# Chunk-selected attention into top-1 routed experts on one core: the last weight piece and two token tiles are sent for sooner, and the last output tile is made in two halves

## The chip, the cores and the metric

The kernel runs on one core of one Trainium2 chip. TensorE (PE) multiplies matrices, and its weight loads are listed apart as PEld. VectorE is DVE, ScalarE is ACT, GpSimd is POOL and SyncE is SP. SP, ACT and POOL also send transfers off; such a row is marked SPq, ACTq or POOLq, or carries the name of a DMA operation, and all transfers run on the same 16 DMA engines. The metric is the device time of one launch in microseconds (us), and lower is better.

## What is computed

The first half is an attention in which each query uses only six chunks of 32 keys, and the second half sends each token through one of eight experts. In the reference, cut to what matters:

```python
ub = sum(maximum(q*k_min[chunk], q*k_max[chunk]))     # bound of each chunk, causal chunks only
top_chunks = argsort(ub)[..., -6:]
attn = softmax(where(sel & causal, q @ k.T / 8, -1e9)) @ v     # 4 batches, 8 heads, 768 tokens, 64 wide
x = attn.transpose(0, 2, 1, 3).reshape(3072, 512)
expert_idx = argmax(x @ w_gate, axis=1)               # 8 experts
for e in range(8):
    xe = x[expert_idx == e]
    out[expert_idx == e] = gate_w * (maximum(xe @ w1[e], 0) @ w2[e])   # 512 -> 1024 -> 512
```

## The kernel before

**Attention.** The work goes by pairs of heads, 16 pairs, four of them to a batch. When the four pairs of a batch are done, a few small steps on DVE choose each token's expert, and six indirect transfers of POOL (line 500, steps `s0` to `s5`) scatter the rows of that batch to a table in DRAM, `xs_dram`, sorted by expert.

**Experts.** The tokens are taken in tiles of 128 rows of one expert. 26 tiles, j = 0 to 25, are always computed. The first 20 are whole tiles; of those the first ten hold rows of the first three batches alone, so they can begin before the last batch is scattered. The last six are made of two halves of 64 rows that belong to two experts. For one tile the steps are:

- `g`: a small transfer, from ACT's queue, of each row's gate and number (line 718);
- `x`: a transposing transfer, from SP's queue, of the tile's rows, 128 by 512 numbers of two bytes (line 743);
- `U`: 16 or fewer matrix products of x with w1 into a two-bank PSUM tile `ph` (line 783);
- `Rl`: ReLU on ACT, from `ph` to the buffer `h` (line 792); there are two buffers `h`;
- `H`: a transposing transfer, from SP's queue, of `h` to `hT` (line 802);
- `D`: products of `hT` with w2 into `py` (line 809), eight for a whole tile and 16, on two halves of the array's columns, for a tile of two experts;
- `Y`: ACT scales `py` by the gate into `y` (line 816);
- `O`: POOL sends the rows of `y` to the output by an indirect transfer (line 820).

**Weights.** w1 and w2 are loaded in 32 pieces of 512 KB by transfers of POOL's queue (line 182, steps `w.0` to `w.31`), which read four-byte numbers and write two-byte ones. `w.26`, `w.14` and `w.30` are the last three that are issued, and all three are pieces of w2. Which expert a whole tile belongs to is known only at run time, so its products read w1 and w2 at an offset from a register. Therefore U.0 waits for every piece of w1, and D.0 for every piece of w2.

**Order.** The text `ORDER` (lines 872 to 943) sets the order of all steps by hand. Each engine issues its instructions, and each queue its transfers, in that order. A transfer takes part in it at the place of its step, so an `x` that stands behind an `H` in the text is issued by SP behind that `H`, which waits for its ReLU. A ReLU writes one of two buffers `h`, so Rl.3 waits until the transfer H.1 has read the buffer that Rl.1 wrote, and Rl.4 until H.2 has.

The waits that the program sets by semaphores, as far as they matter here: U.j waits for x.j and for a free `ph` of three; D.j waits for H.j and for a free `py`; D.0 waits for H.0 and for all of w2; Y.j waits for D.j; O.j for Y.j.

Of the kernel before, what the change touches and what calls it, by code (L numbers as in the profile page):

```python
# [22 lines left out]
def kernel(  # L23
# [18 lines left out]
    DM = H * D  # L42
# [12 lines left out]
    NS = NA + NL + ND + NF2  # L55
# [14 lines left out]
    w2_all = wpool.tile([128, E * WE], BF16)  # L70
# [27 lines left out]
    ps_s = tc.alloc_tile_pool(name="ps_s", bufs=3, space=bass.MemoryType.PSUM)  # L98
    ps_o = tc.alloc_tile_pool(name="ps_o", bufs=1, space=bass.MemoryType.PSUM)
# [17 lines left out]
    for c in range(2):  # L117
# [3 lines left out]
        a = const.tile([128, S], BF16, name=f"IND{c}")  # L121
# [4 lines left out]
    for i in range(2):  # L126
        a = buf.tile([128, 2, 32], FP32, name=f"KK{i}")
# [390 lines left out]
    tag_all = const.tile([128, JT, 2], I32)  # L518
# [161 lines left out]
    NFC = F // 128  # L680
# [5 lines left out]
    fs = [dict() for _ in range(NTILE)]  # L686
# [3 lines left out]
    def kind(j):  # L690
        if j < NA + NL:
            return "whole", j
        if j < NA + NL + ND:
            return "mixed", NFULL + NF2 + j - NA - NL
        if j < NS:
            return "first", NFULL + j - NA - NL - ND
        if j < NS + NB - NL:
            return "whole", NA + NL + j - NS
        return "second", NFULL + NF2 + ND + j - NS - NB + NL
# [103 lines left out]
        fs[j]["hT"] = hT  # L803

    def down_mm(j):
        py = ps_o.tile([128, DM], FP32, tag=("oa", "ob")[j % 2], name="py")
        for c in range(NFC):
            for r, wo in fs[j]["gr"]:
                nc.tensor.matmul(py[r], lhsT=fs[j]["hT"][:, c, r], rhs=w2_all[:, ds(wo + c * DM, DM)],  # L809
                                 start=(c == 0), stop=(c == NFC - 1), skip_group_check=True)  # L810
        fs[j]["py"] = py

    def down_act(j):
        tag, pool, bufs = (("v", ld, LDB["v"]), ("ot", work, 2))[j % 2]
        y = pool.tile([128, DM], FP32, tag=tag, bufs=bufs, name="y")
        nc.scalar.activation(y[:], fs[j]["py"][:], AF.Copy, bias=0.0, scale=tag_all[:, kind(j)[1], 0:1].bitcast(FP32))  # L816
        fs[j]["y"] = y

    def put(j):
# [25 lines left out]
    def sm_c(i):  # L845
# [8 lines left out]
              ra=rb_(r_add), rb=rb_(r_max), rc=rb_(r_shift), rx=rb_(r_exp), rd=rb_(r_cand), re=rb_(r_first),  # L854
              rf=rb_(r_hot), rg=rb_(r_sum), rh=rb_(r_eps), ri=rb_(r_gate), rk=rb_(r_rank), rm=rb_(r_row),
              rn=rb_(r_pick), ro=rb_(r_slot), rp=rb_(r_int),
              g=gather, x=x_in, z=idle_mm, xc=x_tag, U=up_mm, Rl=up_act, H=up_turn, D=down_mm, Y=down_act, O=put, dr=lambda n: nc.gpsimd.drain(), sp=pause, wg=load_gate)
    for u in range(6):
        fn.update({f"sc{u}": sg(sc, u), f"ex{u}": sg(ex, u), f"cm{u}": sg(cm, u), f"av{u}": sg(av, u),
                   f"ac{u}": sg(ac, u), f"s{u}": rb_(r_scat, u)})  # L860

    def steps(gen, n, last):
# [85 lines left out]
    for step in ORDER.split():  # L948
        nm, n = step.split(".")
# [6 lines left out]
    with tc.If(more[0] > 0) as _:  # L956
        for j0 in range(NS, NTILE, 3):
            for j in range(j0, min(j0 + 3, NTILE)):
                gather(j)
                x_in(j)  # L960
                x_tag(j)
            for j in range(j0, min(j0 + 3, NTILE)):
                up_mm(j)
                up_act(j)
                up_turn(j)
            for j in range(j0, min(j0 + 3, NTILE)):
                down_mm(j)
                down_act(j)
                put(j)
# [35 lines left out]
```

## Times and profile before

| what | value |
|---|---|
| time, median of 3 runs | 303.07 us (302.65 to 311.62) |
| profiled execution, its own time | 305.6 us |
| span of its trace, first to last instruction | 303.7 us |
| busy share of PE, DVE, ACT, POOL | 94%, 65%, 62%, 53% |
| granted TensorE clock | 0.998 of full speed |
| bytes moved by the DMA engines | 56.51 MB, 186 GB/s over the span |

All times of rows count from the span's start. PE is busy nearly throughout, so what matters is where it is not, and what it waits for there. The share of busy DMA engines that a view by stretches gives may be above 1, since packets of several queues overlap on an engine.

### The profile page before, as it was taken

How to read it: one execution, taken by the hardware profiler on the slowest of the kernel's cores; microseconds unless marked ns; L12 is line 12 of the kernel's file. 1: busy time of each engine (PE TensorE's matmuls, PEld its weight loads, DVE VectorE, ACT ScalarE, POOL GpSimd, SP SyncE). 2: the span in 40 equal slices, each digit the busy share in tenths (PEclk: the TensorE clock that was granted, in tenths of full speed). 3: DMA queues.
4: the chain of work that ended last, by engine and by line, in shares of the span. 5: the costliest groups of instructions: out<-in, count | busy, mean ns of one | idle time of the engine just before them, and what ended most of it. 6: DMA issues, size and time to landing. Idle time of an engine off the chain costs nothing.

```text
span 303.7 us, 8579 instructions
## 1 busy us (share of the span) xinstructions
PE 285.2 (94%) x3095; PEld 145.3 (48%) x3105; DVE 197.0 (65%) x613; ACT 189.3 (62%) x266; POOL 159.5 (53%) x245
## 2 busy tenths in 40 slices
PE   7899999989999999899999999998699999999992
PEld 3444555454555555555655554453344444444451
DVE  6587988989999988899899899776700322000000
ACT  1978877777777787597877677522435453434541
POOL 5064253553262566635578888413864456753453
PEclk9999999999999999999999999999999999999999
DMA  7999999997989999799999898999997999989872
GB/s 152 201 193 202 201 190 210 177 204 167 208 163 160 191 208 211 149 229 171 189 244 204 159 205 194 106 167 149 224 224 176 208 150 210 235 191 228 139 172 77
DMA packets 132587, 56.51 MB, mean 186 GB/s; under 512 B 121915, under 2 KB 121917, under 8 KB 132544
## 3 DMA queue, kind: packets, MB, share of 16 engines
q1 hardware_dynamic: 117440, 29.13, 52.9%
q0 software_dynamic: 12224, 26.78, 44.8%
q10 hardware_dynamic: 2880, 0.02, 1.4%
q8 instruction: 28, 0.46, 0.6%
q14 instruction: 15, 0.12, 0.1%
HBM read 53.26 MB, written 9.99 MB: 208 GB/s over the span
## 4 chain that ended last, share of the span: by engine, by line
PE 61%; DVE 9%; issue 9%; POOL 6%; DMA 5%; ACT 4%; SPq 3%; POOLq 1%; DVEq 0%; ACTq 0%
PE oa L324 16%; PE ph L783 8%; PE py L809 6%; PE ps L288 6%; DVE Pa L335 5%; PE ps L296 5%; PE pc L242 4%; PE pc L352 4%; POOL out_dram L820 3%; PE ob L324 3%; PE pc L362 2%; DMA KQ<-xg 2%; PE pq L208 2%; PE px L199 2%; DMA x_early<-xs_dram 2%
## 5 line engine op out<-in xcount | busy, mean ns | idle before, releaser
L304 ACT ACTIVATE Pa<-ps 128x1024 f32<-128x1024 f32 x64 | 65.1, 1024 | 15.2 <-PE ps L296 10.0
L335 DVE TENSOR_TENSOR Pa<-Pa 128x1024 f32<-128x1024 f32 (+2 forms) x64 | 64.5, 1008 | 6.9 <-PE oa L324 2.2
L324 PE MATMUL oa<-Pa,v 128*64 128x512 f32 (+2 forms) x320 | 64.3, 518 | 0.0
L311 POOL TENSOR_SCALAR_AFFINE_SELECT Pa<-Pa 128x256 f32<-128x256 f32 x48 | 25.1, 538 | 50.0 <-ACT Pa L304 47.4
L809 PE MATMUL py<-w_all,hT 128*128 (+1 forms) x251 | 46.9, 379 | 1.5 <-issue 1.2
L792 ACT ACTIVATE h<-ph 128x1024 bf16<-128x1024 f32 (+1 forms) x27 | 26.5, 990 | 31.5 <-DMA hT<-h 12.7
L288 PE MATMUL ps<-KQ 64*128 64x512 bf16 (+3 forms) x256 | 37.3, 307 | 1.3 <-ACT Pa L304 0.6
L820 POOL DMA_INDIRECT out_dram<-y,tag_all x26 | 25.7, 989 | 22.9 <-ACT y L816 18.6
L500 POOL DMA_INDIRECT xs_dram<-xrow,sli x24 | 27.8, 1156 | 13.4 <-issue 4.8
L296 PE MATMUL ps<-mt,IND 64*128 64x256 bf16 (+4 forms) x512 | 34.4, 225 | 0.2 <-DVE mt L272 0.2
L809 PEld LDWEIGHTS <-hT 128*128 128x128 bf16 (+1 forms) x256 | 20.8, 102 | 26.0 <-issue 3.3
L816 ACT ACTIVATE y<-py,tag_all 128x512 f32<-128x512 f32 x26 | 17.6, 687 | 21.3 <-PE py L809 19.5
L214 DVE TENSOR_REDUCE KK<-pk 128x24 f32<-128x768 f32 x32 | 29.2, 943 | 1.3 <-PE pk L208 1.2
L324 PEld LDWEIGHTS oa<-Pa,v 128*64 128x64 f32 x320 | 19.4, 136 | 19.8 <-issue 14.7
L783 PE MATMUL ph<-w_all,x_early 128*128 (+1 forms) x125 | 25.3, 379 | 3.0 <-DMA x_early<-xs_dram 2.4
L288 PEld LDWEIGHTS <-KQ 64*128 64x128 bf16 x256 | 13.2, 94 | 28.9 <-issue 28.4
L296 PEld LDWEIGHTS <-IND 64*128 64x128 bf16 x512 | 23.0, 94 | 7.5 <-issue 0.4
L311 POOL TENSOR_SCALAR_AFFINE_SELECT Pb<-Pb 128x256 f32<-128x256 f32 x32 | 20.7, 672 | 9.7 <-ACT Pb L304 8.1
L182 POOL DMA_DIRECT2D w_all<-in_moe_w_dram x32 | 23.9, 748 | 0.1
L752 DVE TENSOR_TENSOR tag_all<-tag_all,inv_i 128x1 int32<-128x1 int32 x10 | 1.5, 158 | 31.8 <-DMA tag_all<-xs_dram 28.5
L783 PE MATMUL ph<-w_all,KQ 128*128 (+1 forms) x127 | 21.9, 380 | 0.1
L226 ACT ACTIVATE qN<-pq 128x576 f32<-128x576 f32 x16 | 10.4, 652 | 15.4 <-PE pq L208 15.4
(167 smaller groups left out, 449.7 us busy)
## 6 DMA issues: line engine op xcount, KB each, us to landing
w_all<-in_moe_w_dram POOLq DMA_DIRECT2D x32, 512.0 KB
k<-in_k_dram SPq DMA_DIRECT2D x32, 192.0 KB
q<-in_q_dram SPq DMA_DIRECT2D x32, 192.0 KB
v<-in_v_dram SPq DMA_DIRECT2D x32, 192.0 KB
hT<-h SPq DMA_TRANSPOSE x27
out_dram<-y,tag_all POOLq DMA_INDIRECT x26
xs_dram<-xrow,sli POOLq DMA_INDIRECT x24
tag_all<-xs_dram ACTq DMA_DIRECT2D x20, 1.0 KB
```

The source lines that it names most:

```text
L214: nc.vector.tensor_reduce(KK[i % 2][:, n, 0:NCH], st[i]["pk"].rearrange("p (c w) -> p c w", w=CH), AX.X, ALU.max if n == 0 else ALU.min, n ...
L288: nc.tensor.matmul(ps[:, hd, ds(c0, w)], lhsT=kc_[r, ts(kb_, 128)], rhs=qc_[r, ds(q0, w)], start=True, stop=False, skip_group_check=True)
L296: nc.tensor.matmul(o[:, :, c, :], lhsT=IND[c][r, ts(kb_, 128)], rhs=mt[r, ds(j0, n), :], start=False, stop=True, skip_group_check=True)
L304: nc.scalar.activation(P[:], st[i][f"ps{u}"][:, :, 0:w], AF.Exp)
L311: nc.gpsimd.affine_select(out=pd, in_=pd, pattern=[[0, 2], [1, 128]], compare_op=ALU.is_ge, fill=0.0, base=0, channel_multiplier=-1)
L324: nc.tensor.matmul(po[64 * hd:64 * hd + 64, ds(q0 - o0, w)], lhsT=vt[:, kb_, hd, :], rhs=P[:, hd, ds(c0, w)], start=(u <= 1 and n == 0), s ...
L335: nc.vector.tensor_tensor(a[:, :, ds(q0_, w)], a[:, :, ds(q0_, w)], P[:, :, ds(c0, w)], ALU.add)
L500: d = nc.gpsimd.indirect_dma_start(out=xs_dram[:], out_offset=bass.IndirectOffsetOnAxis(ap=sli[:, u:u + 1], axis=0), in_=bst[b]["xrow"][:, ...
L783: nc.tensor.matmul(ph[r, fh, :], lhsT=fs[j]["xT"][:, c, r], rhs=w1_all[:, ds(wo + c * F + fh * 512, 512)], start=(c == 0), stop=(c == NDC ...
L792: nc.scalar.activation(h_[:, a].rearrange("q a (c j p) -> q (a c) j p", c=2, j=2), fs[j]["ph"][:, a].rearrange("q a (c p j) -> q (a c) j p ...
L809: nc.tensor.matmul(py[r], lhsT=fs[j]["hT"][:, c, r], rhs=w2_all[:, ds(wo + c * DM, DM)], start=(c == 0), stop=(c == NFC - 1), skip_group_c ...
L820: d = nc.gpsimd.indirect_dma_start(out=out[:], out_offset=bass.IndirectOffsetOnAxis(ap=tag_all[:, kind(j)[1], 1:2], axis=0), in_=fs[j]["y" ...
```

## The change

Three edits. In the text of the order, `w.30` stands right behind `w.14` now, ahead of three steps of POOL's own (`lga`) that it was behind; and `x.5` and `x.6` each stand one `H` further ahead: x.5 ahead of H.1 (it was behind H.2), x.6 between H.1 and H.2 (it was behind x.5, behind both). And the last tile's products, j = 25, are computed in two halves of 256 columns, each half in a PSUM bank of its own, from the pool that `ph` comes from; ACT scales each half by itself. There are 32 products of 256 columns in place of 16 of 512, so 16 more weight loads, and two ACT instructions in place of one. The output transfer O.25 stays one.

```diff
     def down_mm(j):
-        py = ps_o.tile([128, DM], FP32, tag=("oa", "ob")[j % 2], name="py")
-        for c in range(NFC):
-            for r, wo in fs[j]["gr"]:
-                nc.tensor.matmul(py[r], lhsT=fs[j]["hT"][:, c, r], rhs=w2_all[:, ds(wo + c * DM, DM)],
-                                 start=(c == 0), stop=(c == NFC - 1), skip_group_check=True)
-        fs[j]["py"] = py
+        if j == NS - 1:
+            ends = ps_s.tile([128, 2, 512], FP32, tag="s", name="py")
+            fs[j]["py"] = ends[:, :, 0:DM // 2]
+        else:
+            fs[j]["py"] = ps_o.tile([128, DM], FP32, tag=("oa", "ob")[j % 2], name="py")[:].unsqueeze(1)
+        n = fs[j]["py"].shape[2]
+        for a in range(DM // n):
+            for c in range(NFC):
+                for r, wo in fs[j]["gr"]:
+                    nc.tensor.matmul(fs[j]["py"][r, a], lhsT=fs[j]["hT"][:, c, r],
+                                     rhs=w2_all[:, ds(wo + c * DM + a * n, n)],
+                                     start=(c == 0), stop=(c == NFC - 1), skip_group_check=True)
 
     def down_act(j):
...
-        nc.scalar.activation(y[:], fs[j]["py"][:], AF.Copy, bias=0.0, scale=tag_all[:, kind(j)[1], 0:1].bitcast(FP32))
+        n = fs[j]["py"].shape[2]
+        for a in range(DM // n):
+            nc.scalar.activation(y[:, ds(a * n, n)], fs[j]["py"][:, a], AF.Copy, bias=0.0,
+                                 scale=tag_all[:, kind(j)[1], 0:1].bitcast(FP32))
...
-        av4.15 av5.15 xr.13 xt.14 ac0.15 lga.13 ac2.15 w.14 Rl.0 ut.14 rcp.14 sm.15 lgt.14 g.1 ocA.15 gt.15 xr.14
-        lga.14 uc.15 g.2 xt.15 ut.15 rcp.15 g.3 lgt.15 g.4 U.1 lga.15 xr.15 ra.15 rb.15 H.0 rc.15 rx.15 rd.15 U.2
-        rg.15 x.4 re.15 rh.15 rf.15 Rl.1 Rl.2 U.3 rk.15 w.30 H.1 ri.15 rm.15 H.2 rn.15 x.5 ro.15 rp.15 U.4 Rl.3 x.6
+        av4.15 av5.15 xr.13 xt.14 ac0.15 lga.13 ac2.15 w.14 w.30 Rl.0 ut.14 rcp.14 sm.15 lgt.14 g.1 ocA.15 gt.15
+        xr.14 lga.14 uc.15 g.2 xt.15 ut.15 rcp.15 g.3 lgt.15 g.4 U.1 lga.15 xr.15 ra.15 rb.15 H.0 rc.15 rx.15 rd.15
+        U.2 rg.15 x.4 x.5 re.15 rh.15 rf.15 Rl.1 Rl.2 U.3 rk.15 H.1 x.6 ri.15 rm.15 H.2 rn.15 ro.15 rp.15 U.4 Rl.3
         Rl.4 x.7 s0.15 D.0 H.3 D.1 s1.15 Y.0 Y.1 tB.0 tB.1 g.5 g.6 g.7 s2.15 H.4 sp.0 U.5 D.2 Rl.5 s3.15 U.6 g.8
```

SP's queue at the start of the expert stage, before. The rows are x.4, H.1, H.2, x.5, x.6, x.7 and H.3; an ISA row sets the address of the x behind it.

```order
L743 DMA_TRANSPOSE x_early_3718<-xs_dram_63 128x4x128
L802 DMA_TRANSPOSE hT_3881<-h_3851 128x8x128
L802 DMA_TRANSPOSE hT_3887<-h_3853 128x8x128
L743 ISA
L743 DMA_TRANSPOSE x_early_3718<-xs_dram_63 128x4x128
L743 ISA
L743 DMA_TRANSPOSE KQ0_124<-xs_dram_63 128x4x128
L743 ISA
L743 DMA_TRANSPOSE KQ0_124<-xs_dram_63 128x4x128
L802 DMA_TRANSPOSE hT_3926<-h_3908 128x8x128
```

The same place of SP's queue in the changed kernel: x.4, x.5, H.1, x.6, H.2, x.7, H.3.

```order
L743 DMA_TRANSPOSE x_early_3718<-xs_dram_63 128x4x128
L743 ISA
L743 DMA_TRANSPOSE x_early_3718<-xs_dram_63 128x4x128
L802 DMA_TRANSPOSE hT_3882<-h_3853 128x8x128
L743 ISA
L743 DMA_TRANSPOSE KQ0_124<-xs_dram_63 128x4x128
L802 DMA_TRANSPOSE hT_3889<-h_3855 128x8x128
L743 ISA
L743 DMA_TRANSPOSE KQ0_124<-xs_dram_63 128x4x128
L802 DMA_TRANSPOSE hT_3926<-h_3909 128x8x128
```

So H.1 has one more x ahead of it and H.2 two; from x.7 on the queue is as it was.

POOL at the same time: the pieces of weights are the rows of line 182, `lga` is line 408, and the scatters of the last batch are line 500.

```order
 L182 DMA w_all<-in_moe_w_dram 128x2x1024
 L408 TENSOR_TENSOR lg<-lg,lgt 128x96
-L182 DMA w_all<-in_moe_w_dram 128x2x1024
+L182 DMA w_all<-in_moe_w_dram 128x2x1024 x2
 L408 TENSOR_TENSOR lg<-lg,lgt 128x96 x2
-L182 DMA w_all<-in_moe_w_dram 128x2x1024
 L500 DMA xs_dram<-xrow,sli 24576x258 x3
```

w.30 has left its place between the two `lga` and the scatters and is the second of the pair behind the first `lga`. PE and DVE keep their order but for the last tile.

## Rows read from the trace of the kernel before

**Rows 1.** Waits of TensorE, 196 to 300 us: total, times, longest (us).

```profile
PE ph L783 <- DMA x_early<-xs_dram: 2.4, 2, 1.8
PE py L809 <- issue: 1.2, 1, 1.2
```

**Rows 2.** Timeline of TensorE: start, length (us), engine, line, tile, count [idle before].

```profile
210.13 1.89 PE L783 MATMUL ph<-w_all,x_early 128*128 x8 [0.31 <-issue]
213.26 3.62 PE L809 MATMUL py<-w_all,hT 128*128 x15 [1.25 <-issue]
218.71 1.89 PE L783 MATMUL ph<-w_all,x_early 128*128 x8 [1.83 <-DMA x_early<-xs_dram]
220.43 1.89 PE L809 MATMUL py<-w_all,hT 128*128 x8
...
225.61 3.62 PE L809 MATMUL py<-w_all,hT 128*128 x15
```

**Rows 3.** Line 809 by itself, waits before weight loads: ns min/median/max, first and last start.

```profile
L809 PEldq EVENT_SEMAPHORE  x2: 51/990/1929, 211.1 to 211.2; - x2
```

**Rows 4.** Timeline of POOL, 196 to 212 us.

```profile
197.26 0.73 POOL L182 DMA_DIRECT2D w_all<-in_moe_w_dram  x1
202.84 0.38 POOL L408 TENSOR_TENSOR lg<-lg,lgt 128x96 f32<-128x96 f32 x1 [4.84 <-DVE lgt L400]
...
205.53 0.72 POOL L182 DMA_DIRECT2D w_all<-in_moe_w_dram  x1
```

**Rows 5.** Timeline of SP's queue in several stretches, 200 to 216 us.

```profile
202.51 3.26 SPq L743 DMA_TRANSPOSE x_early<-xs_dram  x1
207.62 1.24 SPq L802 DMA_TRANSPOSE hT<-h  x1
...
207.62 4.85 SPq L802 DMA_TRANSPOSE hT<-h  x2
212.63 1.19 SPq L743 DMA_TRANSPOSE x_early<-xs_dram  x1
213.96 2.53 SPq L743 DMA_TRANSPOSE KQ<-xs_dram  x2
```

**Rows 6.** Timeline of ACT, 206 to 222 us.

```profile
206.59 1.01 ACT L792 ACTIVATE h<-ph 128x1024 bf16<-128x1024 f32 x1
...
214.01 1.02 ACT L792 ACTIVATE h<-ph 128x1024 bf16<-128x1024 f32 x1 [5.09 <-DMA hT<-h]
216.03 1.02 ACT L792 ACTIVATE h<-ph 128x1024 bf16<-128x1024 f32 x1 [0.99 <-DMA hT<-h]
...
221.67 1.02 ACT L792 ACTIVATE h<-ph 128x1024 bf16<-128x1024 f32 x1 [3.46 <-DMA tag_all<-xs_dram]
```

**Rows 7.** Stretches: length, busy PE, PEld, DVE, ACT, POOL, clock, DMA share, GB/s.

```profile
198.50:205.50 7.00, 6.70 (x80) 3.69 (x80) 5.44 (x16) 2.11 (x3) 0.77 (x2) 1.00 1.22 180
...
211.50:212.50 1.00, 0.52 (x3) 0.02 (x1) 0.86 (x6) 0.00 (x0) 0.69 (x2) 1.00 0.05 5
```

**Rows 8.** Timeline of the end, 289 to 304 us.

```profile
289.31 8.80 PE L809 MATMUL py<-w_all,hT 128*64 x80
...
298.20 0.69 ACT L816 ACTIVATE y<-py,tag_all 128x512 f32<-128x512 f32 x1 [1.04 <-PE py L809]
299.16 0.97 POOL L820 DMA_INDIRECT out_dram<-y,tag_all  x1 [0.76 <-ACTq L956]
```

**Rows 9.** Groups by form, ACT: count, busy us, mean ns, idle before.

```profile
L816 ACT ACTIVATE y<-py,tag_all 128x512 f32<-128x512 f32 x26 | 17.6, 687 | 21.3 <-PE py L809 19.5 <-issue 1.7
L343 ACT ACTIVATE ot<-oa 128x512 f32<-128x512 f32 x16 | 9.6, 601 | 0.7 <-PE oa L324 0.7
L341 ACT ACTIVATE ot<-ob 128x256 f32<-128x256 f32 x16 | 6.4, 398 | 0.0
```

**Rows 10.** Timeline: products of 256 columns, and two loads of 64 columns.

```profile
184.02 0.38 PE L296 MATMUL ps<-mt,IND 64*128 64x256 bf16 x4
...
288.88 0.11 PEld L783 LDWEIGHTS <-x_early 128*64 128x64 bf16 x2
```

## Prediction, written before the changed kernel was run

> **What bounds the kernel now.** I began with the page's busy shares, which put TensorE far ahead of the others, and so asked for TensorE's own waits. From 196 us on, where the experts begin, there are three of any size: two for token tiles and one of 1.2 us in the products with w2 that the view can't name [rows 1]. The timeline gives their places [rows 2]. U.4 starts at 210.13 and ends at 212.02. D.0 starts only at 213.26: that is the wait of 1.25 us. D.0 and D.1 take 1.73 us each and end at 216.88; U.5 starts at 218.71, 1.83 us later, held by x.5. Behind it TensorE goes on without a gap that counts, so work that starts sooner here ends the kernel sooner, if nothing else comes late.
>
> **What D.0 waits for.** One of two waits ahead of line 809's weight loads lasts 1929 ns from 211.2, so until 213.13 [rows 3]. D.0 needs H.0 and all of w2. H.0 was issued long before; the last piece, w.30, was issued at 205.53 [rows 4]. The DMA engines stand nearly still from 211.5 to 212.5 [rows 7], which fits a piece whose bytes have been moved and whose completion is still to come. I take w.30 as the cause, by elimination.
>
> **What x.5 waits for.** SP issues it at 212.63, behind H.1 and H.2 [rows 5]. H.1 can't start before Rl.1 ends, at 207.60 [rows 6], and takes 1.24; the two together take 4.85, so H.2 alone has some 3.5, against 1.24 when nothing holds it. x.4 was slow too, 3.26, and both times weight pieces were moving. In between, from 205.77 to 207.62, SP waits for Rl.1 with nothing to do.
>
> **When the H land.** This isn't recorded, but ACT shows it: Rl.3 reuses the buffer that H.1 reads and starts at 214.01, Rl.4 that of H.2 at 216.03, both held by "DMA hT<-h" [rows 6]. H.1 thus lands at about 213.95, and D.1, which needs it, starts at 214.99 (213.26 and 1.73) [rows 2]. D.1 has 1.0 us to spare, no more. This is the number that decides.
>
> **The change, part by part.**
>
> *w.30 behind w.14.* POOL issues it at 198.0 (197.26 and 0.73) and waits for DVE from there until 202.84 [rows 4], so its 0.72 us of POOL hides in that wait; if the wait were gone, `lga.14` would be later by 0.72 and nobody would notice before the last batch's routing. Nothing waits for the place at 205.53 that it leaves. Its bytes stand behind w.26 and w.14 in the same queue. The engines move 180 GB/s in all from 198.5 to 205.5 [rows 7], 1.26 MB, of which those two pieces alone are 1.05 MB beside token tiles and H.0, so w.30 starts to flow 0 to 2 us sooner, not 7.5. D.0 then starts between 212.02, the end of U.4, and 213.26 as now: a gain of 0 to 1.25 by itself.
>
> *x.5 ahead of H.1.* Its price on SP is between 1.19, its own length now, and 3.26, that of x.4 just ahead of it with pieces moving [rows 5]. x.4 is the nearer in place, the other the nearer in that SP's queue has had time to empty; I take the middle, 2.1. From 205.9 that ends at 208.0, so H.1 is issued 0.4 late. Its 131 KB (128 by 512 by 2 bytes) go ahead of H.1's at 180 GB/s, 0.73 us. H.1 lands at 213.95 + 0.4 + 0.73 = 215.1. D.1 starts then, whether D.0 began at 212.02 or at 213.26: what w.30 gives is lost in the wait for H.1. The other end is 213.75, H.1 no obstacle and D.0 at 212.02.
>
> *U.5* then follows D.1 at once: 215.1 + 1.73 = 216.85 in place of 218.71, a gain of **1.86**. Its `ph` is free after Rl.3, at 215.1 + 1.0, in time. x.5 has been on its way since 206 and is no longer late.
>
> *x.6 ahead of H.2.* H.2 landed at 216.0; with the bytes of x.5 and x.6 ahead, 1.46 us, at 217.5. D.2 needs it at 216.85 + 1.73 = 218.6: covered, with 1.1 to spare. If that cover were gone, each microsecond would show one for one. x.7 and H.3 have the same transfers ahead of them as before; H.3 landed by 221.67, when Rl.5 got its buffer [rows 6], and D.3 would want it at 225.61 - 1.86 = 223.75 [rows 2]. So the gain is kept. Behind this the transfers follow TensorE's own steps and move with it.
>
> *The last tile in halves.* TensorE: five tiles of 16 products take 8.80 [rows 8], 110 ns a product, two side by side. 32 products of 256 columns cost the same if they take 55 ns. Four of 256 columns with a load each took 0.38 [rows 10], of which the length of one such product is most, so about 53 ns apart: I take 0 extra. ACT's part behind the last product, 0.69 now [rows 8], is a half. A plain copy of 512 columns takes 601 and of 256 columns 398 [rows 9], so halving saves 203 ns; bounds are 0 (the first half waits for the last product after all) and 0.34 (half of 687). I take **0.20**. O.25 and its landing stay.
>
> **Sum.** 1.86 + 0.20 = 2.06 us. The profiled execution took 305.6, of which 303.7 span and 1.9 around it: 303.5. The median is 303.07, 2.5 under the profiled one, near the lower of the runs (302.65): less 2.06 that is **301.0**.
>
> **The rivals.**
>
> *All of it (0.18).* H.1 isn't delayed, because w.30 is out of its way sooner and x.5 fits SP's empty 1.85 us. Then D.0 starts at 212.02, D.1 at 213.75 to 213.95 and U.5 at 215.5 to 215.7: 3.0 to 3.2, with the end 3.2 to 3.4, about 299.7. For it: 1.19 is the commoner length. Against: the same bytes move on engines whose share is above 1 all the while [rows 7].
>
> *Little of it (0.17).* x.5 takes 3.26 as x.4 did, until 209.2, and H.1 behind it 3.5 as H.2 did, until 212.7. H.2 landed 3.5 after its issue ended (212.47 to 216.0), so H.1 lands at 216.2, U.5 starts at 217.95: 0.75, with the end 0.95, so 302.1.
>
> *Slower (0.12).* x.5 meets what H.2 met: SP is held until 212.47, when the pieces have gone. H.1 is issued from 212.6 to 213.85 and lands 3.5 to 4 later, at 217.4 to 217.85. The point that decides is 216.98 (218.71 less 1.73): an H.1 later than that is a loss. U.5 starts 0.4 to 0.9 late, and H.2, behind x.6, makes D.2 wait as much again at worst. Less 0.20, it is 0.2 to 1.5 over, about 303.9. For it: two transfers of SP's queue in four were held here. Against: SP has 1.85 us to spare there.
>
> *Weight loads in the open (0.06).* Two loads of 64 columns take 0.11 [rows 10]. If the 16 added ones don't run beside products, the last tile takes 8 times 0.11 = 0.88 longer; with 1.86 and 0.20 gained, 301.9. Against: 16 products with 16 loads come at 110 ns, little over what the columns need, so today's loads are hidden [rows 8]. The Trainium skill (TensorE: Matmul & The Clock Gate, "The mechanism" under "Part 3: Packing small matmuls — row/col tiling") has a rule for this rival: a weight load overlaps products in flight only when it goes to another group of rows, and all loads here use all 128 rows. By that rule the 0.88 is paid; by the trace it isn't, for loads on all rows are hidden in every tile now.
>
> The forecast keeps 0.47.
>
> **Range and chances.** All cases but part of the slower one lie from 299.7 to 303.6; with 0.3 of scatter at the lower end the range is **299.4 to 303.6**. A measurement of this kernel tells about 2%, 6 us, from no change. No case reaches 6 us either way, so within 2% has 0.95, and what is left, faster 0.02 and slower 0.03, is for what I haven't thought of.
>
> **What would show it.** D.0's wait at line 809 shorter; x.5's row on SP at about 205.9 and its length between 1.2 and 3.3; Rl.3, which tells when H.1 lands, at about 215.2; TensorE waiting for H.1 between D.0 and D.1; U.5 at about 216.85 without a wait for its tile; ACT's last instruction some 0.48 long. Wrong would be Rl.3 behind 217, or D.0 still waiting past 213.3 with w.30 issued at 198: then the wait was never for w.30.

## The result, and the profile after

The changed kernel takes 305.02 us (median of 19 runs, 303.03 to 311.34), the kernel before, beside it on the same chip, 303.05 (19 runs, 301.05 to 311.62). The ratio is 1.0065 with a 95% interval of 1.0044 to 1.0086: about 2.0 us slower, where 2.1 us faster was forecast. The profiled execution of the changed kernel took 304.1 us, span 302.2, mean granted clock 0.993, less than that of the kernel before (305.6, span 303.7): one execution of each would have told the wrong sign.

TensorE's waits from 196 to 300 us in the changed kernel, to be laid beside [rows 1]:

```profile
PE ph L783 <- DMA x_early<-xs_dram: 1.8, 1, 1.8
PE py L815 <- ACT y L824: 1.5, 1, 1.5
```

The wait of 1.2 without a name is gone, and so is one of the two for token tiles. A new one, for ACT's `y`, has come. TensorE's timeline, beside [rows 2], tells which they are (line 815 is line 809 of before, and 824 is 816):

```profile
196.67 1.89 PE L783 MATMUL ph<-w_all,x_early 128*128 x8
203.10 3.61 PE L783 MATMUL ph<-w_all,x_early 128*128 x16
208.56 1.89 PE L783 MATMUL ph<-w_all,x_early 128*128 x8 [1.85 <-DMA x_early<-xs_dram]
210.59 1.89 PE L783 MATMUL ph<-w_all,x_early 128*128 x8
212.31 3.62 PE L815 MATMUL py<-w_all,hT 128*128 x16
215.77 1.89 PE L783 MATMUL ph<-w_all,x_early 128*128 x8
219.19 1.89 PE L815 MATMUL py<-w_all,hT 128*128 x8 [1.53 <-ACT y L824]
221.23 3.61 PE L783 MATMUL ph<-w_all,KQ 128*128 x16 [0.16 <-issue]
```

From the top: U.0; U.1 and U.2; U.3, which now waits 1.85 for x.3; U.4; D.0 and D.1 without a wait; U.5 without a wait; D.2, which now waits 1.53 for Y.0; U.6 and U.7.

Why x.3 is late is to be seen in three rows: POOL's timeline (w.14 and w.30 in one row), the chain of waits (start, length, what), and SP's timeline, where H.0 stands in front of x.4 and x.5:

```profile
196.14 1.45 POOL L182 DMA_DIRECT2D w_all<-in_moe_w_dram  x2
```

```profile
196.75 11.28 DMA x_early<-xs_dram
...
213.19 4.25 DMA hT<-h
```

```profile
199.68 4.53 SPq L802 DMA_TRANSPOSE hT<-h  x1
204.35 3.21 SPq L743 DMA_TRANSPOSE x_early<-xs_dram  x2
209.62 2.13 SPq L802 DMA_TRANSPOSE hT<-h  x1
211.89 1.19 SPq L743 DMA_TRANSPOSE KQ<-xs_dram  x1
213.19 1.24 SPq L802 DMA_TRANSPOSE hT<-h  x1
```

x.3 is issued at 196.75, in the midst of w.14 and w.30, and lands 11.28 us later, at 208.03. H.0 takes SP 4.53, where it took 1.58 in the kernel before (and H.1 1.24, [rows 5]). How the third piece holds x.3 is to be seen in the packets that the DMA engines moved. Queue q0 is POOL's, with the weight pieces in packets of 2 KB. Queue q1 is SP's, where the 131 KB of an x go in 512 packets of 256 bytes. These are the packets, MB and shares from 202 to 206 us, while w.14 and w.30 flow, and below them those from 208 to 209, when no piece is left:

```profile
q0 software_dynamic: 363, 0.71, 93.6%
q1 hardware_dynamic: 365, 0.09, 17.4%
...
q1 hardware_dynamic: 1041, 0.26, 131.8%
```

Beside a piece the two queues move packet for packet, about 91 a us each, and so they do elsewhere (after_third, 210 to 214 us: 360 and 358; same_again, 202 to 204: 175 and 172). Alone, SP's queue moves 1041 in one us. From these rows I estimate that an x would need 512 / 91 = 5.6 us with a piece beside it all the time, and half a us without one. The third piece keeps a piece beside x.3 until past 206 us; in same_again the two that flow there have gone by 204.4.

Behind H.1 stands x.6 (the KQ row, 211.89), and H.2 can go only at 213.19. ACT's timeline shows what hangs on both, beside [rows 6]:

```profile
202.19 6.21 ACTq L718 DMA_DIRECT2D tag_all<-xs_dram  x3
208.59 1.92 ACT L792 ACTIVATE h<-ph 128x1024 bf16<-128x1024 f32 x2
213.16 1.02 ACT L792 ACTIVATE h<-ph 128x1024 bf16<-128x1024 f32 x1 [2.66 <-DMA hT<-h]
217.54 1.02 ACT L792 ACTIVATE h<-ph 128x1024 bf16<-128x1024 f32 x1 [3.35 <-DMA hT<-h]
218.46 0.68 ACT L824 ACTIVATE y<-py,tag_all 128x512 f32<-128x512 f32 x1
```

Rl.4 (217.54) waits until H.2 has landed (213.19 + 4.25 = 217.44). Y.0 stands behind it on ACT, at 218.46, and D.2 writes the `py` that Y.0 reads: it starts at 219.19. The first row is a side effect. In the list of instructions with their waits, g.2, g.3 and g.4 wait for the semaphores of x.0, x.1 and x.2 in the kernel before and for those of x.1, x.2 and x.3 in the changed one, since moving x.5 shifts the turn of the eight semaphores that these transfers share. So ACT is held until x.3 has landed, and Rl.1, H.1 and x.6 start later.

The end, beside [rows 8], TensorE, ACT and POOL:

```profile
287.64 8.82 PE L815 MATMUL py<-w_all,hT 128*64 x96
```

```profile
296.55 0.84 ACT L824 ACTIVATE y<-py,tag_all 128x256 f32<-128x256 f32 x2 [1.06 <-PE py L815]
```

```profile
297.67 0.97 POOL L829 DMA_INDIRECT out_dram<-y,tag_all  x1 [0.93 <-ACTq L965]
```

The halves cost TensorE nothing (8.82 against 8.80). But from TensorE's end to the last put it is 297.67 - 296.46 = 1.21, where it was 299.16 - 298.11 = 1.05.

### The profile page after: what moved, and what is told of

The parts are those of the page before. It is cut to its first block, busy times and chain, and to the rows that moved or that the text cites. A ratio compares the mean times of both kernels' runs of the same rounds, so it can differ in the third digit from the quotient of the medians.

```text
span 302.2 us, 8622 instructions
## 1 busy us (share of the span) xinstructions
PE 286.1 (95%) x3121; PEld 146.1 (48%) x3121; DVE 197.8 (65%) x613; ACT 189.2 (63%) x267; POOL 158.2 (52%) x245
## 4 chain that ended last, share of the span: by engine, by line
PE 61%; DVE 12%; DMA 8%; issue 5%; SPq 5%; ACT 4%; POOL 4%; ACTq 0%; POOLq 0%; DVEq 0%
PE oa L324 12%; PE py L815 11%; PE ph L783 11%; DVE Pa L335 6%; PE ps L288 5%; PE pc L242 5%; DMA x_early<-xs_dram 4%; PE ps L296 4%; PE pc L352 3%; PE ob L324 2%; DVE KK L214 2%; SPq L743 2%; DMA k<-in_k_dram 2%; POOL out_dram L829 2%; PE pq L208 2%
## 5 line engine op out<-in xcount | busy, mean ns | idle before, releaser
L335 DVE TENSOR_TENSOR Pa<-Pa 128x1024 f32<-128x1024 f32 (+2 forms) x64 | 65.2, 1019 | 6.2 <-PE oa L324 1.9
L815 PE MATMUL py<-w_all,hT 128*128 (+3 forms) x272 | 47.2, 367 | 1.5 <-ACT y L824 1.5
L792 ACT ACTIVATE h<-ph 128x1024 bf16<-128x1024 f32 (+1 forms) x27 | 26.5, 990 | 27.5 <-DMA hT<-h 14.3
L500 POOL DMA_INDIRECT xs_dram<-xrow,sli x24 | 26.9, 1120 | 16.2 <-DVE cnt L527 7.6
L815 PEld LDWEIGHTS <-hT 128*128 128x128 bf16 (+1 forms) x272 | 21.6, 103 | 25.7 <-issue 3.3
L824 ACT ACTIVATE y<-py,tag_all 128x512 f32<-128x512 f32 (+1 forms) x27 | 17.8, 670 | 21.3 <-PE py L815 20.0
L783 PE MATMUL ph<-w_all,KQ 128*128 (+2 forms) x128 | 21.9, 380 | 0.2 <-issue 0.2
L226 ACT ACTIVATE qN<-pq 128x576 f32<-128x576 f32 x16 | 10.4, 653 | 15.3 <-PE pq L208 15.3
```

The source lines that it names most:

```text
L335: nc.vector.tensor_tensor(a[:, :, ds(q0_, w)], a[:, :, ds(q0_, w)], P[:, :, ds(c0, w)], ALU.add)
L500: d = nc.gpsimd.indirect_dma_start(out=xs_dram[:], out_offset=bass.IndirectOffsetOnAxis(ap=sli[:, u:u + 1], axis=0), in_=bst[b]["xrow"][:, ...
L783: nc.tensor.matmul(ph[r, fh, :], lhsT=fs[j]["xT"][:, c, r], rhs=w1_all[:, ds(wo + c * F + fh * 512, 512)], start=(c == 0), stop=(c == NDC ...
L792: nc.scalar.activation(h_[:, a].rearrange("q a (c j p) -> q (a c) j p", c=2, j=2), fs[j]["ph"][:, a].rearrange("q a (c p j) -> q (a c) j p ...
L815: nc.tensor.matmul(fs[j]["py"][r, a], lhsT=fs[j]["hT"][:, c, r], rhs=w2_all[:, ds(wo + c * DM + a * n, n)], start=(c == 0), stop=(c == NFC ...
```

## The result across executions: the measure for the experiments

Times of two equal kernels differ here by about as much as the edits are worth, so each experiment is also read by a distance within its own trace: from U.0's start to U.8's. The executions begin U.0 between 196 and 207 us, the late ones at a mean granted clock of 0.98 to 0.99; within the stretch a tile takes 1.73 us of TensorE in all of them, so only distances from U.0 are compared. Without any wait the distance would be 27.5 to 28.3 (each row less its waits). "Third piece" is where the last of w.26, w.14, w.30 stands: late (behind rk.15, as before) or early. Ratios are to the kernel before, run beside it on the same chip.

```
kernel          third piece  x.6       waits of TensorE, U.0 to U.8       U.0 to U.8  ratio (95%)
before          late         old       U.4 .31, D.0 1.25, U.5 1.83        31.30
same_again      late         old       D.0 1.60                           29.42       1.0026 (0.9995-1.0057)
halves_only     late         old       D.1 .38, U.5 1.00                  29.17       1.0018 (0.9964-1.0072)
x_only          late         ahead     D.1 .81, D.2 .51                   29.39       1.0036 (0.9989-1.0083)
x_halves        late         ahead     D.0 1.40                           29.01       1.0004 (0.9967-1.0042)
y0_x_halves     late         ahead     U.1 .15, U.2 .79                   28.89       1.0044 (1.0008-1.0080)
x5_halves       late         old       D.0 1.86                           29.48       1.0035 (0.9993-1.0077)
w_swap          late (w.14)  ahead     D.0 .51, D.1 .34                   28.42       1.0026 (0.9990-1.0063)
x5_swap         late (w.14)  old       D.0 1.21                           28.83       1.0016 (0.9979-1.0053)
no_w30          none         ahead     D.2 1.44, U.6 .20                  29.41       0.9975 (0.9937-1.0013)
no_w30_x_back   none         old       U.5 1.65                           29.26       0.9978 (0.9937-1.0019)
x5_no_w30       none         old       U.1 .32, U.8 .33                   28.14       0.9950 (0.9905-0.9995)
after           early        ahead     U.3 1.85, D.2 1.53, U.6 .16        31.47       1.0065 (1.0044-1.0086)
after_again     early        ahead     U.3 .83, D.2 1.30                  30.32       1.0015 (0.9979-1.0052)
after_third     early        ahead     U.3 1.88, D.2 1.53                 31.49       1.0062 (1.0025-1.0099)
w_only          early        old       U.3 2.26, U.5 .35, D.4 .86         31.73       1.0012 (0.9966-1.0058)
w_mid           early        ahead     U.1 .24, U.4 2.98, D.2 .74         31.69       0.9972 (0.9916-1.0027)
w_fourth        early        ahead     U.3 .91, U.4 1.28, D.2 .80         31.01       1.0064 (1.0019-1.0109)
```

The first row, on which the prediction rests, is the only one with a late third piece that is longer than 29.5. All eight ratios with a late third piece lie above 1, at 1.0026 in the mean, and that of the unchanged kernel is among them: a ratio of this size can come from the measure itself.

## The experiments

Edits of the order are given as the few steps around the place. The expectations speak of three theories. A: w.30 right behind w.14 puts three pieces in a row on the DMA engines, and they hold the token tiles back. B: x.5 and x.6 ahead of H.1 and H.2 make Rl.4, Y.0 and so D.2 late. C: the loss is elsewhere, in the halves, in the stages ahead, or in the clock.

**same_again: the kernel before once more, unchanged.**

> The kernel before, unchanged, as one more kernel of the row. It shows how far two equal kernels stand apart (0 expected, an interval of some 0.3% either way), what clock their executions have in the records, and how much the attention stage and the start of the expert stage differ from one profile to the next.

```profile
213.56 3.61 PE L809 MATMUL py<-w_all,hT 128*128 x16 [1.60 <-issue]
217.21 1.89 PE L783 MATMUL ph<-w_all,x_early 128*128 x8
```

TensorE again: D.0 waits 1.60, and U.5 doesn't wait at all. Against itself the kernel reads 1.0026, which is what such a ratio can be off by.

**halves_only: the two functions of the change, the order of before.**

```diff
-lga.13 ac2.15 w.14 w.30 Rl.0
+lga.13 ac2.15 w.14 Rl.0
-x.4 x.5 re.15 ... rk.15 H.1 x.6 ri.15 rm.15 H.2 rn.15 ro.15
+x.4 re.15 ... rk.15 w.30 H.1 ri.15 rm.15 H.2 rn.15 x.5 ro.15 ... Rl.3 x.6
```

> Only the last tile's down product in two halves. Theories A and B: the last scaling on ACT is 0.28 us shorter behind the last product, so 0.2 to 0.3 us faster. Theory C: 1 to 2 us slower, with the loss either at the end or in the first 30 us, where the order is the same but the program's code is longer.

A third execution of the old order, 29.17, with waits of 0.38 and 1.00 (the second named as ACT's `y`). At the end ACT's pair takes 0.84 again and the put comes 1.20 us behind TensorE's end (297.13 - 295.93).

**x_only: x.5 and x.6 moved, nothing else.**

```diff
-rg.15 x.4 re.15 ... H.1 ri.15 rm.15 H.2 rn.15 x.5 ro.15 ... Rl.3 x.6
+rg.15 x.4 x.5 re.15 ... H.1 x.6 ri.15 rm.15 H.2 rn.15 ro.15 ... Rl.3
```

> x.5 behind x.4 and x.6 between H.1 and H.2, w.30 where it was. Theory A: x.3 lands as before, so ACT's tag transfers, which now stand behind x.3 in place of x.2, are not held; U.5 starts at once behind D.1: 1 to 2 us faster. Theory B: H.2 lands late, Rl.4 and Y.0 with it, and D.2 waits for Y.0 as in the changed kernel (1.53 us): between 0.5 faster and 1 us slower. Theory C: no difference beyond 0.3 us.

```profile
217.93 1.89 PE L809 MATMUL py<-w_all,hT 128*128 x8
220.63 1.89 PE L809 MATMUL py<-w_all,hT 128*128 x8 [0.81 <-DMA hT<-h]
222.35 1.89 PE L783 MATMUL ph<-w_all,x_early 128*128 x8
224.75 1.89 PE L809 MATMUL py<-w_all,hT 128*128 x8 [0.51 <-ACT y L816]
```

D.0, D.1, U.5, D.2: the wait for x.5 is away, D.1 now waits for H.1, as forecast, and D.2 for Y.0. The stretch, 29.39, is that of the old order, and the time isn't told from it either (1.0036, with 0.5% to either side).

**w_only: w.30 moved, nothing else.**

```diff
-ac2.15 w.14 Rl.0 ... rk.15 w.30 H.1
+ac2.15 w.14 w.30 Rl.0 ... rk.15 H.1
```

> w.30 behind w.14, nothing else changed. Theory A (three weight pieces in a row hold the token tiles back: x.3 and x.4 land later, U.3 waits for x.3 as in the changed kernel, 1.85 us): U.3 waits 1 to 2 us, D.0 no longer waits for w.30, x.5 still late behind H.2: 0.5 to 1.5 us slower than before. Theory B (the loss comes from x.5 and x.6 standing ahead of H.1 and H.2, so Rl.4 and Y.0 are late and D.2 waits): this kernel has none of it and is 0 to 1.2 us faster. Theory C (the loss is not in this stage at all, but in the halves or in the first 30 us): no difference beyond 0.3 us.

```profile
214.35 1.89 PE L783 MATMUL ph<-w_all,x_early 128*128 x8 [2.26 <-DMA x_early<-xs_dram]
```

```profile
205.06 4.83 SPq L802 DMA_TRANSPOSE hT<-h  x1
207.56 1.35 ACTq L718 DMA_DIRECT2D tag_all<-xs_dram  x3
```

TensorE, SP and ACT: U.3 waits 2.26 for x.3, which SP issues at 202.62 and which lands some 11.2 us later; H.0 takes 4.83; D.0 doesn't wait. ACT's tag transfers take 1.35 here and hold nothing: the shared semaphores aren't what makes x.3 late. The whole time doesn't show the loss (1.0012, with 0.5% to either side).

**after_again: the changed kernel on another chip.** No edit.

> The changed kernel once more, beside the kernel before on one chip with every run's clock. If the loss of 0.65% is the kernel's and not the clock's, it is 1 to 2 us slower than before among executions of equal clock, and its profile has U.3 waiting 1.5 us or more for x.3 again, with U.6 starting about 24.5 us after U.0 against 22.3 to 22.5 in the two ordinary profiles of the kernel before. If the first profile was chance, U.3 does not wait and U.6 starts 22 to 23 us after U.0.

U.3 waits 0.83, less than the 1.5 that was expected, and D.2 1.30; U.6 starts 23.42 behind U.0, between the two forecasts. The loss is 0.15% here, and its interval holds zero.

**x_halves: the changed kernel with w.30 back.**

```diff
-ac2.15 w.14 w.30 Rl.0 ... rk.15 H.1
+ac2.15 w.14 Rl.0 ... rk.15 w.30 H.1
```

> The changed kernel with w.30 back in its old place alone. Theory A (w.30 right behind w.14 makes the loss): U.3 does not wait, U.6 starts 22.3 to 22.8 us after U.0, and the time is 1.5 to 2.2 us less than the changed kernel's, within 0.7 of the kernel before. Theory B (x.5 and x.6 ahead of H.1 and H.2 make it): no more than 0.5 us less than the changed kernel.

```profile
213.48 3.61 PE L815 MATMUL py<-w_all,hT 128*128 x16 [1.40 <-issue]
...
218.66 1.89 PE L815 MATMUL py<-w_all,hT 128*128 x8
```

U.3's wait is gone and D.0's is back. It hides what H.2's delay would cost at D.2. The time is a miss: 1.0004 here and 1.0015 for the changed kernel on the same chip are 0.1% apart, and 1.5 to 2.2 us, 0.5 to 0.7%, were expected.

**w_early: the kernel before with w.30 right behind w.3, from 7.8 us behind U.0 to 10.4 ahead of it.**

```diff
-av2.14 w.3 av3.14 ... rk.15 w.30 H.1
+av2.14 w.3 w.30 av3.14 ... rk.15 H.1
```

> The kernel before with w.30 right behind w.3, 7 us ahead of w.26, at 189 us, where the DMA engines are busy 0.6 to 0.9 of the time in place of 1 and more. Theory A in its narrow form (what hurts is a third piece in a row behind w.26 and w.14, while x.2 to x.4 and H.0 are in the queue): U.3 does not wait, D.0 does not wait, and the time is 0 to 1.2 us less than before. In its wide form (any piece moved ahead of the token tiles holds them back): U.0 or U.1 starts 1 to 2 us late for its tile, and the time is 0 to 1.5 us more.

The stretch takes 29.95 with one wait of 2.35 at U.5; neither U.3 nor D.0 waits. Its six runs lie at 306.85 and from 311.49 to 317.12, too few and too far apart for a ratio to the kernel before (median 307.11). Whether it is slower stays open.

**y0_x_halves: x_halves with D.0 and Y.0 ahead of Rl.4.**

```diff
-U.4 Rl.3 Rl.4 x.7 s0.15 D.0 H.3 D.1 s1.15 Y.0 Y.1
+U.4 Rl.3 D.0 Y.0 Rl.4 x.7 s0.15 H.3 D.1 s1.15 Y.1
```

> As x_halves, and Y.0, which frees the PSUM tile that D.2 writes, ahead of Rl.4 on ACT, which waits for H.2. If D.2's wait for Y.0 (0.5 us with the tiles moved alone, 1.5 in the changed kernel) is what keeps the two token tiles from paying, D.2 starts at once behind U.5 and U.6 starts 0.5 us sooner after U.0 than in x_halves; the time is 0.3 to 0.8 us less than x_halves. If H.1's landing ahead of D.1 sets the pace alone, there is no difference beyond 0.3 us.

28.89 and no wait at D.2, but x_halves has none there either, so this run doesn't test the repair. Waits of 0.39 and 0.96 follow at D.5 and D.6, and the kernel is not faster (1.0044). U.2 waits 0.79 for x.2, which lands 10.73 us after its issue with no third piece near: a token tile can be as late by chance.

**no_w30: the changed kernel without the load of w.30.** That part of w2 is filled with zeros at the start.

```diff
-    nc.gpsimd.memset(dcol[:], 0.0)
+    nc.gpsimd.memset(dcol[:], 0.0); nc.vector.memset(w2_all[:, ds(7 * WE, 4 * DM)], 0.0)
-ac2.15 w.14 w.30 Rl.0
+ac2.15 w.14 Rl.0
```

> The changed kernel with w.30 left out: its half megabyte isn't loaded, and that part of w2 is filled with zeros at the start by VectorE, so the products with those weights are zero. Everything else as changed. Theory A (the third piece in a row holds the token tiles back): U.3's wait for x.3, 1.85 and 0.83 us in two profiles of the changed kernel, is gone, H.0's row on SP is about 1.3 to 1.6 long as in the kernel before, and from U.0's start to U.8's it takes 28.0 to 29.0 us, where the changed kernel takes 31.47 and 30.32; the time is 1.5 to 2.5 under the changed kernel's, so about equal to the kernel before or 0.5 under it. Theory B (x.5 and x.6 ahead of H.1 and H.2 make Rl.4, Y.0 and D.2 late): D.2 still waits 1.3 to 1.5 for Y.0, U.0 to U.8 about 30. Also: if D.0's wait in the kernel before was for w.30, D.0 waits for nothing here.

```profile
210.69 5.34 PE L783 MATMUL ph<-w_all,x_early 128*128 x24
...
217.90 3.62 PE L815 MATMUL py<-w_all,hT 128*128 x16
...
224.67 1.89 PE L815 MATMUL py<-w_all,hT 128*128 x8 [1.44 <-ACT y L824]
```

U.1 to U.3 run in one piece, H.0 takes 1.61, and neither U.3 nor D.0 waits; D.2 does. Both theories were right, each for its own wait; the stretch, 29.41, is over A's 28.0 to 29.0, since it holds D.2's wait.

**no_w30_x_back: the same with x.5 and x.6 at their old places.**

```diff
-x.4 x.5 re.15 ... H.1 x.6 ri.15 rm.15 H.2 rn.15 ro.15 ... Rl.3 Rl.4
+x.4 re.15 ... H.1 ri.15 rm.15 H.2 rn.15 x.5 ro.15 ... Rl.3 x.6 Rl.4
```

> w.30 left out in the same way, and x.5 and x.6 back at the places of the kernel before; the last down product in halves stays. With w.30 out of the picture this tells what the moved token tiles are worth by themselves. The prediction's second step: without the move U.5 waits for x.5 (1.83 in the first profile of the kernel before), so U.0 to U.8 is 1.5 to 1.9 longer than with the move. What the later profiles speak for: the wait for x.5 is the exception, and U.0 to U.8 is the same within 0.5 with and without the move, 28.0 to 29.0. If the wait for x.5 came from w.30's bytes, it is gone here too.

```profile
210.90 3.62 PE L815 MATMUL py<-w_all,hT 128*128 x16
216.16 1.89 PE L783 MATMUL ph<-w_all,x_early 128*128 x8 [1.65 <-DMA x_early<-xs_dram]
```

Without w.30 the wait for x.5 is real, 1.65, and the move exchanges it for 1.44 at D.2: 29.26 against 29.41. My guess that it was only an exception fell: it shows in full where D.0 hasn't waited first, and in the kernel before it came on top of D.0's.

**w_mid: w.30 behind lga.14 (201.67 in this trace).**

```diff
-ac2.15 w.14 w.30 Rl.0 ... xr.14 lga.14 uc.15
+ac2.15 w.14 Rl.0 ... xr.14 lga.14 w.30 uc.15
```

> The changed kernel with w.30 issued behind the routing add of the 15th pair, about 202.5 instead of 197.3 or 205.5 (in times of a profile whose U.0 starts near 197). Theory A: w.14 and w.26 have gone by, x.3 and H.0 are ahead of it, so U.3 doesn't wait; w.30 lands some 3 us sooner than in the kernel before, so D.0 doesn't wait either; U.0 to U.8 28.2 to 29.0, and the time is 0.5 to 1.0 under the kernel before. Theory B: D.2 waits for Y.0 1.0 to 1.5 and U.0 to U.8 is 29.5 to 30.5.

```profile
211.33 1.89 PE L783 MATMUL ph<-w_all,x_early 128*128 x8 [2.98 <-DMA x_early<-xs_dram]
```

```profile
196.77 8.18 DMA x_early<-xs_dram
```

TensorE and the chain of waits. A miss: x.3 lands in 8.18 us and U.3 is free, as expected, but x.4, whose issue begins at 200.76 and lasts beyond that of the piece, holds U.4 for 2.98. That the piece does this is not shown: from 206 to 208 us of this execution the DMA engines move 39 GB/s in all, where they move some 200 beside a piece otherwise, and one execution doesn't tell why. The whole time shows no loss (0.9972).

**w_fourth: w.3 loaded a second time right behind w.30.**

```diff
-ac2.15 w.14 w.30 Rl.0
+ac2.15 w.14 w.30 w.3 Rl.0
```

> The changed kernel with the suspected cost doubled: right behind w.30 the piece w.3, long in place, is loaded once more, a fourth half megabyte in a row. Theory A: at some 180 GB/s the fourth piece adds up to 2.9 us of bytes in front of the last token tiles, so U.3's wait grows from 0.8 to 1.9 to 3 to 5 us, H.0's row on SP to 6 or more, and the time is 2 to 4 over the changed kernel's. Theory B or C (the loss is elsewhere): U.3's wait stays under 2.5 and the time is that of the changed kernel.

```profile
206.25 11.04 DMA x_early<-xs_dram
```

```profile
q0 software_dynamic: 465, 0.89, 93.8%
q1 hardware_dynamic: 462, 0.12, 17.4%
```

A miss, and by what was expected it spoke against A: x.3 lands in 11.04 us, as with three pieces, U.3 waits 0.91, not 3 to 5, and U.4 waits 1.28 for ACT; H.0 takes 3.86. The expectation had put the fourth piece's bytes in front of x.3. The packets, here from 211 to 216 us, show another way: the queues move one for one again, so x.3 has its 512 turns and lands at 217.28 while POOL's queue is still at work (84 packets from 217 to 218). More pieces hold an x only as long as it has packets left. The order of the issues is not the reason: the fourth piece's begins 0.3 us behind that of x.3, but in the changed kernel w.30's began 0.1 us behind it and did hold it. The Trainium skill (DMA: Bandwidth & Descriptors, "Queues, rings and completion order") says that a DMA engine takes turns between the queues that have work for it, packet by packet. The counts of both queues, 465 and 462, agree, if what the trace counts as a packet is what the page means.

**x5_halves: the kernel before with x.5 alone ahead of H.1, and the halves.**

```diff
-rg.15 x.4 re.15 ... H.2 rn.15 x.5 ro.15
+rg.15 x.4 x.5 re.15 ... H.2 rn.15 ro.15
```

> The kernel before with x.5 alone ahead of H.1 (x.6 stays behind Rl.3, w.30 stays behind rk.15), and the halves. If it is x.6 ahead of H.2 that makes H.2, Rl.4, Y.0 and so D.2 late, U.5 waits for nothing, D.2 for nothing, and what is left is D.0's wait of 0 to 1.6 for w.30: U.0 to U.8 28.0 to 29.0, and the time 0.5 to 1.0 under the kernel before. If x.5's place alone does it, D.2 still waits 0.8 to 1.5 for Y.0 and the time is that of the kernel before.

D.0 waits 1.86 and nothing else does, 29.48. The time, 1.0035, is not under that of the kernel before.

**x5_no_w30: the same without w.30** (zeros in its place). The added lines of no_w30, and:

```diff
-rk.15 w.30 H.1
+rk.15 H.1
```

> The same without w.30 (that part of w2 is zeros). Beside the two earlier kernels without w.30, where U.5 waited 1.65 for x.5 or D.2 waited 1.44 for Y.0, only x.6's place differs from the second. If x.6 ahead of H.2 is the cause of D.2's wait: neither wait, U.0 to U.8 27.6 to 28.2, 1.2 to 1.7 shorter than in both, and the time 1 us under theirs. If not: D.2 waits 1.0 to 1.5 again and U.0 to U.8 is 29 to 29.5.

```profile
216.05 3.62 PE L815 MATMUL py<-w_all,hT 128*128 x15
219.50 1.89 PE L783 MATMUL ph<-w_all,x_early 128*128 x8
221.23 1.89 PE L815 MATMUL py<-w_all,hT 128*128 x8
```

D.0 to D.2 without a gap, 28.14. Beside no_w30 only x.6's place differs: x.6 ahead of H.2 is what makes D.2 wait, as far as one execution of each tells. It is also the only kernel whose interval lies below 1 (0.9905 to 0.9995), but half a megabyte of weights isn't loaded.

**w_swap: the changed kernel with w.14 in w.30's old place.**

```diff
-ac2.15 w.14 w.30 Rl.0 ... rk.15 H.1
+ac2.15 w.30 Rl.0 ... rk.15 w.14 H.1
```

> The changed kernel with w.14 in w.30's old place: w.26 and w.30 in a row, and w.14 behind rk.15. If it is the third piece in a row, whichever it is, that holds the token tiles: U.3 doesn't wait for x.3, H.0's row is 1.2 to 1.6, and U.0 to U.8 is that of the order with w.30 in its old place, 28.9 to 29.4; the time is 1.5 us under the changed kernel's. If w.30's own bytes or place were the cause, U.3 waits 0.8 to 2.3 as in the changed kernel.

```profile
203.68 1.58 SPq L802 DMA_TRANSPOSE hT<-h  x1
207.10 5.34 PE L783 MATMUL ph<-w_all,x_early 128*128 x23
214.98 1.67 PE L815 MATMUL py<-w_all,hT 128*128 x7 [0.51 <-issue]
```

w.30 stands behind w.26 here, no third piece follows, and U.1 to U.3 don't wait. So it is the third in a row, not w.30. The last piece, now w.14, holds D.0 for 0.51.

**x5_swap: x.5 alone ahead of H.1, the two pieces exchanged, the halves.**

```diff
-ac2.15 w.14 w.30 Rl.0 ... rk.15 H.1 x.6 ri.15
+ac2.15 w.30 Rl.0 ... rk.15 w.14 H.1 ri.15
-ro.15 rp.15 U.4 Rl.3 Rl.4
+ro.15 rp.15 U.4 Rl.3 x.6 Rl.4
```

> What the runs so far point to, put together: the kernel before with x.5 alone ahead of H.1, x.6 left where it was, w.30 right behind w.26 and w.14 in w.30's old place, and the halves. If the two causes are the third piece in a row and x.6 ahead of H.2, no wait is left but that of D.0 for the last piece, 0 to 1.9: U.0 to U.8 is 28.0 to 29.6, where three profiles of the order before have 29.2 to 31.3 and three with the changed order 30.3 to 31.7; the time is 0.5 to 1.5 under the kernel before and 2 under the changed one. The other theory, that the chain's end is set elsewhere and the stage's gain is given back behind U.8: U.0 to U.8 short, the time that of the kernel before within 0.3 per cent.

**after_third: the changed kernel beside it.** No edit.

> The changed kernel itself, on the same chip as the kernel before it in this list, for the two to be compared. By the theory: U.3 waits 0.8 to 2.3 for x.3, D.2 waits 1.3 to 1.5 for Y.0, U.0 to U.8 30.3 to 31.7, the time 0.2 to 0.7 per cent over the kernel before. If the stage is as short as in the kernels with two pieces in a row (under 29.5), the two earlier profiles of the changed kernel were the exception.

```profile
204.03 11.66 DMA x_early<-xs_dram
...
216.21 1.89 PE L783 MATMUL ph<-w_all,x_early 128*128 x8 [1.88 <-DMA x_early<-xs_dram]
...
226.84 1.89 PE L815 MATMUL py<-w_all,hT 128*128 x8 [1.53 <-ACT y L824]
```

The changed kernel repeats itself: x.3 lands in 11.66 us, U.3 waits 1.88 and D.2 1.53, 31.49, and there is a loss again (1.0062, interval 1.0025 to 1.0099). x5_swap has neither wait, 28.83, and is level with the kernel before (1.0016). Its median is 303.86, that of the changed kernel on this chip 305.55; worked out between these two, the changed kernel takes 0.5% more, with an interval from 0.2 to 0.8%. These two, on one chip, differ by both causes, the third piece in a row and x.6 ahead of H.2, and else only by which piece is the last: with both taken back the loss is gone. The 0.5 to 1.5 us under the kernel before that were expected didn't come. No order that loads all the weights is shown to beat the kernel before.

## Why the prediction was wrong, step by step

*The base.* The prediction took the waits of one profiled execution, 305.6 us long, from a median of 303.07. That execution had both the wait at D.0 and that at U.5 in full, 31.30 from U.0 to U.8. Two other executions of the same order have 29.42 and 29.17, what the prediction wanted to reach (31.30 less 1.86 is 29.44): in same_again D.0's wait of 1.60 gave x.5 the time to come. In these two the 1.86 was not there to be gained. The 2.5 us between profile and median, which I named, could have been a reason to look at a second execution; they are no measure of the stretch, since same_again took 305.87 with 29.42.

*w.30 behind w.14.* This step failed: "Nothing waits" was true of POOL, and the bytes were counted only for when w.30 itself would flow; what they cost x.3 was put at nothing. They flow beside x.3, which then lands 10.4 to 11.7 us after its issue (7.9 to 9.1 in the executions with two pieces), and U.3 waits 0.83 to 2.26 in the four executions that have w.30 right behind w.14 and no fourth piece. That D.0 waits for w.30 was right: it is gone wherever w.30 is early or left out, and comes with the last piece late in six executions of nine (0.51 to 1.86). But the wait at U.3 came in its place and is as long. The prediction's price for 131 KB ahead in the queue, 0.73 us at 180 GB/s, went by bytes; beside a piece the queues take turns by packets, and an x would need some 5.6 us.

*x.5 ahead of H.1.* That U.5 no longer waits for x.5 was forecast rightly. That it starts 19.10 us behind U.0, where 216.85 - 197.76 = 19.09 was forecast, is luck, for the way there was another: U.3's 1.85 took the place of D.0's 1.25 and U.4's 0.31, and D.1 did not wait for H.1, the wait that the forecast turned on. Rl.3, which tells of H.1's landing, starts at 213.16, and D.1 some 0.9 later. So of the rival "slower", which had the sign right, the first cause, a late H.1, did not come; the second, H.2 behind x.6, did.

*x.6 ahead of H.2.* This step failed too: "covered" was wrong. I asked when D.2 needs H.2 itself, and not who else waits for its landing: Rl.4 does, Y.0 stands behind Rl.4 on ACT, and D.2 needs the buffer that Y.0 empties. With 1.30 us more in front of H.2 on SP (211.89 to 213.19) D.2 waited 1.53. All of what U.5 had gained was gone at U.6, 24.56 behind U.0, where it had been 24.40. x5_no_w30, where the wait is gone with x.6 back behind H.2, shows the cause. That H.1 itself went 12.95 behind U.0 (9.86 before), since ACT was held, adds to this in the changed kernel, but isn't needed for it: in no_w30 H.1 goes at 10.36 and D.2 waits 1.44.

*The halves.* Forecast 0.20 gained, measured 0.16 lost (1.21 against 1.05). TensorE's part was right: 16 products and 16 loads more for 0.02 us. The line of the Trainium skill (TensorE: Matmul & The Clock Gate, "The mechanism" under "Part 3: Packing small matmuls — row/col tiling") that the prediction drew on would have a load on the same rows not overlap, and so 0.88 more by the prediction's estimate; the trace has 0.02 and doesn't agree. The same section also lets a load into the background weight buffer overlap, which the prediction left out. ACT's part fell to the lower bound that I had named. In the instruction list the second half carries no wait of its own, the first has the only one for TensorE, and it starts at 296.55, behind TensorE's end at 296.46: both halves wait for the whole tile, and two copies take 0.84 where one took 0.69.

*How much is shown.* The two new waits, the edits that make them and the end's 0.16 are shown by the traces. The stretch of the old order is about 29.3 in two executions of three, that of the changed one 31.5 in two of three, which is near the 2.0 us that were measured. That both causes together make the loss rests on x5_swap beside after_third. That the whole time follows the stretch is not shown edit by edit: w_only and w_mid have long stretches and no loss, w_swap a short one and no gain, and from U.8 to the end the executions differ by 74.1 to 78.3 us. Nor did I settle why the loss was 0.65% and 0.62% on two chips and 0.15% on a third.

## What to carry to other kernels

Look at a wait in two or three executions before you count on removing it; two waits in one chain can cover each other, and here the sum of both was there in one execution of three. When a transfer is issued sooner, ask which small transfers share the DMA engines with it in the new place, and count their packets, not their bytes; when one is put in front of another in a queue, follow everything that waits for the second one's landing, also through another engine's order. A split of the last copy gained nothing here, where its first half has no wait of its own but that for the whole tile: the list of instructions shows that before any run.

## What the runs showed that I had not expected

- The transposing load x.3, 131 KB, lands 10.4 to 11.7 us after its issue with three half-megabyte pieces in a row on POOL's queue (11.28, 10.38, 11.66 and 11.21 in after, after_again, after_third and w_only) and 7.9 to 9.1 with two, and the next transposing transfer's issue, H.0, takes 3.5 to 4.8 us of SP in place of 1.2 to 1.9. A fourth piece behind them adds nothing (11.04).
- Beside a weight piece SP's queue moves one packet of 256 bytes for each packet of 2 KB of the piece, about 91 a us, and 1041 in one us without a piece: 0.09 MB in 4 us against 0.26 MB in 1.
- Moving one transfer on SP's queue made three others on ACT's queue wait for later transfers (6.21 us in place of 2.10), since all of them take turns at the same eight semaphores.
